# Two uneven groups of tokens, 384 and 512, in place of two batches of 448 in the two layers behind attention

## The chip, the cores and the metric

The kernel runs on one core of a Trainium2 chip. TensorE (PE in the profile) does the matmuls; VectorE (DVE), ScalarE (ACT) and GpSimd (POOL) do the work between them; SyncE (SP) issues the transfers. The metric is the device time of one execution in microseconds (us), lower is better.

## What is computed

Causal attention (2 batches, 12 heads, 448 positions, 64 wide) gives 896 tokens of 768 numbers. Two layers follow, on all 896 tokens:

```python
def _moe_ref(x, w_in, w_out, a, b):          # 768 -> 2048 -> 768
    h = x @ w_in
    P = a[0] + a[1] * h + a[2] * h**2 + a[3] * h**3
    Q = 1.0 + np.abs(b[0]) * np.abs(h) + np.abs(b[1]) * h**2
    return (P / (Q + 1e-06)) @ w_out

def _moe2_ref(x, w_gate, w_val, w_out):      # 768 -> 1536 -> 768
    gate = 1.0 / (1.0 + np.exp(-(x @ w_gate)))
    return (gate * (x @ w_val)) @ w_out
```

## The kernel before

Every number of the layers is kept as a high and a low part, and each product is three matmuls: high by high, high by low, low by high. A matmul has 128 x 128 weights (or, in the last product, 128 x 128 of the tokens' numbers) that stand still, and a moving operand of so many columns. For all products but the last the columns are tokens: 448 of them, one batch.

The first layer goes in four chunks `c` of 512 of the 2048 inner numbers. Stage in(c, b) makes four tiles `h` of 128 inner numbers for batch `b` (6 steps of 3 matmuls each, 72 in all, lines 239 to 241); the function `rational` then works on each tile on ACT and DVE, and POOL makes the low part `gl` (line 271). Stage out(c, b) multiplies them by `w_out` into six tiles `o` (4 steps of 3 matmuls each, 72 in all, lines 295 to 297), which DVE adds to the sums `y1` (line 305; in chunk 0 ACT copies them). After the last chunk ACT and POOL write the sums as `xh` and `xl`, the second layer's input.

The second layer goes in six chunks of 256 inner numbers. Stage in2(c, b) makes tiles `gu` (gate) and `vu` (value), 18 matmuls each, two of each kind per stage. Stage out2(c, b) makes tiles `z`, whose moving operand is 384 columns of weights, 6 matmuls each: six tiles for tokens 0 to 383 (b = 0), eight for the rest (b = 1).

The order of the work on each engine is written out by a planner: each piece is a `Job` with an engine, a cost, what it waits for and a rank, and `in_turn` plays them through. All matmuls stand in one chain, in the order of the stages: in(0,0), out(0,0), in(0,1), in(1,0), out(0,1), in(1,1), out(1,0), in(2,0) and so on to in(3,1), out(3,0); then in2(0,0) woven into out(3,1), in2(0,1), and from there out2(c,0), in2(c+1,0), out2(c,1), in2(c+1,1). Six PSUM banks take the matmuls' results in turn.

Of the kernel before, what the change touches and what calls it, by code (L numbers as in the profile page):

```python
# [69 lines left out]
def tile_causal_attention__moe_rational__moe_glu(  # L70
# [26 lines left out]
    NT = B * S  # L97
# [10 lines left out]
    tmp = ctx.enter_context(tc.tile_pool(name="tmp", bufs=3))  # L108
# [10 lines left out]
    for i in range(N_WARM):  # L119
# [7 lines left out]
        out=mask[:, S - CP :],  # L127
# [88 lines left out]
    YW = 4 * DM  # L216
    ypools = [y_a, None]

    ready = [0] + [(b + 1) * S // P for b in range(B)]
    y1 = {}  # L220
    y2 = {}
    wt = {}
# [4 lines left out]
    def psum_tile(nm, n=S):  # L227
        if "b" not in bank:
            return ps_a.tile([P, 512], F32, tag="mm", name=nm)[:, :n]
        nmm[0] += 1  # L230
        pool = ps_a if nmm[0] % 6 < 2 else bank["b"]
        return pool.tile([P, 512], F32, tag="mm", name=nm)[:, :n]

    def up(ps, w, fo, b):
        hi, lo = w
        bs = slice(b * S, (b + 1) * S)
        fs = slice(fo, fo + P)
        for c in range(KC):
            nc.tensor.matmul(ps, hi[:, c, fs], xh[:, c, bs], start=(c == 0), stop=False)  # L239
            nc.tensor.matmul(ps, hi[:, c, fs], xl[:, c, bs], start=False, stop=False)  # L240
            nc.tensor.matmul(ps, lo[:, c, fs], xh[:, c, bs], start=False, stop=(c == KC - 1))  # L241
            yield

    def rational(ps, gh, gl, nm):
        t = tmp.tile([P, S], F32, tag="t0", name=f"t_{nm}")
        z = tmp.tile([P, S], F32, tag="t1", name=f"z_{nm}")

        if "d" in bank:
            d = bank["d"].tile([P, 512], F32, tag="d", name=f"d_{nm}")[:, :S]
        else:  # L250
            d = tmp.tile([P, S], F32, tag="t2", name=f"d_{nm}", bufs=2)

        nc.scalar.activation(z, ps, AF.Square)
        nc.scalar.activation(d, ps, AF.Abs, scale=b_sb[:, 0:1])
        nc.scalar.activation(t, ps, AF.Identity, bias=a_sb[:, 2:3], scale=a_sb[:, 3:4])
        yield
        nc.vector.scalar_tensor_tensor(z, z, nb[:, 1:2], d, op0=ALU.mult, op1=ALU.subtract)
        nc.vector.tensor_tensor(t, t, ps, op=ALU.mult)
        nc.vector.scalar_tensor_tensor(t, t, a_sb[:, 1:2], ps, op0=ALU.add, op1=ALU.mult)
        yield  # L260

        nc.scalar.activation(d, z, AF.Ln, bias=one, scale=-1.0)
        nc.scalar.activation(d, d, AF.Exp, scale=-1.0)
        yield
        nc.vector.scalar_tensor_tensor(t, t, a_sb[:, 0:1], d, op0=ALU.add, op1=ALU.mult)
        nc.vector.scalar_tensor_tensor(d, z, one, d, op0=ALU.subtract, op1=ALU.mult)
        nc.vector.scalar_tensor_tensor(t, d, 2.0, t, op0=ALU.add, op1=ALU.mult)
        yield
        nc.scalar.copy(gh, t)  # L269
        yield  # L270
        nc.gpsimd.tensor_tensor(gl, t, gh, op=ALU.subtract)  # L271

    def in1_tile(c, b, i):

        nm = f"h{c}_{b}_{i}"
        if i % 2 == 0:
            for t in ("gh", "gl"):
                g[t, c, b, i // 2] = gpools[b].tile([P, 2, S], F32R, tag=t, name=f"{t}_{nm}")
        gh, gl = (g[t, c, b, i // 2][:, i % 2] for t in ("gh", "gl"))
        g[c, b, i] = gh, gl  # L280
        ps = psum_tile(nm)
        return up(ps, wt["in", c, i // 2], (i % 2) * P, b), rational(ps, gh, gl, nm)

    def out1_tile(c, b, e):

        if c == 0 and e == 0:
            y1[b] = ypools[b].tile([P, YW], F32, tag="y", name=f"y1_{b}")
        ps = psum_tile(f"o{c}_{b}_{e}")

        def products():  # L290
            es = slice(e * P, (e + 1) * P)
            for i in range(NF):
                hi, lo = wt["out", c, i]
                gh, gl = g[c, b, i]
                nc.tensor.matmul(ps, hi[:, es], gh, start=(i == 0), stop=False)  # L295
                nc.tensor.matmul(ps, hi[:, es], gl, start=False, stop=False)  # L296
                nc.tensor.matmul(ps, lo[:, es], gh, start=False, stop=(i == NF - 1))  # L297
                yield

        def follows():  # L300
            yy = y1[b][:, e * S : (e + 1) * S]
            if c == 0:
                nc.scalar.copy(yy, ps)
            else:
                nc.vector.tensor_tensor(yy, yy, ps, op=ALU.add)
            if c == NCH - 1:
                yield
                x = (slice(None), e, slice(b * S, (b + 1) * S))
                nc.scalar.copy(xh[x], yy)
                yield  # L310
                nc.gpsimd.tensor_tensor(xl[x], yy, xh[x], op=ALU.subtract)

        return products(), follows()

    def gate_tile(c, b, i):
        g["gate"] = psum_tile(f"gu{c}_{b}_{i}")
        return up(g["gate"], wt["gate", c, 0], i * P, b), None

    def val_tile(c, b, i):

        nm = f"u{c}_{b}_{i}"
        if b == 0:
            g["l2", c, i] = [gpools[c % 2].tile([P, NT], F32R, tag=t, name=f"{t}2_{c}_{i}") for t in ("gh", "gl")]
        gh, gl = (t[:, b * S : (b + 1) * S] for t in g["l2", c, i])
        pg = g["gate"]
        pv = psum_tile(f"v{nm}")

        def follows():
            sg = tmp.tile([P, S], F32, tag="t0", name=f"sg_{nm}")
            pr = tmp.tile([P, S], F32, tag="t1", name=f"pr_{nm}")  # L330
            nc.scalar.activation(sg, pg, AF.Sigmoid)
            yield
            nc.vector.tensor_tensor(pr, sg, pv, op=ALU.mult)  # L333
            yield
            nc.scalar.copy(gh, pr)  # L335
            yield
            nc.gpsimd.tensor_tensor(gl, pr, gh, op=ALU.subtract)  # L337

        return up(pv, wt["val", c, 0], i * P, b), follows()

    def out2_tile(c, m, n):

# [271 lines left out]

    job("late", "", 0.0, [k for k in J if k != "ab"], 0, late)

    UNIT, UNIT2 = 0.615, 0.52

    STAGES = [("SP", 4.0), ("ACT", 0.92), ("ACT", 0.9), ("DVE", 1.3), ("ACT", 0.84), ("POOL", 2.0)]
    portions = []  # L620
# [90 lines left out]
    GLU = [("ACT", 0.62), ("DVE", 0.62), ("ACT", 0.56), ("POOL", 1.25)]  # L711

    def stage_in(c, b):

        groups = [(0, 1), (2,), (3,)] if (c, b) == (0, 0) else [(i,) for i in range(NF)]
        for group in groups:
            keys = [("in", c, b, i) for i in group]
            deps = [place(k, 1) for k in keys]
            for u in range(KC):
                for k, d in zip(keys, deps):  # L720
                    w = [("in", c, k[3] // 2, u // 3, 5), ("lo", b * NP + u)]
                    matmuls(k, u, d + w, UNIT, in1_tile)
# [142 lines left out]
```

## Time and profile before

| | |
|---|---|
| time, median of 3 runs | 609.58 us (609.33 to 610.33) |
| the profiled execution | 614.51 us |
| its span, first to last instruction | 612.5 us |
| PE busy | 604.6 us, 99% of the span |
| DVE, ACT, POOL busy | 357.9, 356.8, 256.6 us |

The profiled execution is one, taken with the hardware profiler on, and 0.8% longer than the median; times inside the kernel come from it. An engine that is busy 99% of the span is not at its peak for that: matmuls are pipelined, and a matmul's listed duration overlaps the next one's.

### The profile page before, as it was taken

Reading aid. Unit: us, or ns where it says so; the run is one execution under the profiler, and the core shown is the slowest. Engines: PE = TensorE matmul, PEld = TensorE weight load, DVE = VectorE, ACT = ScalarE, POOL = GpSimd, SP = SyncE. Lnnn points to the kernel's source line nnn. Section 1 sums busy time; section 2 is a strip of 40 time slices with the busy share of each in tenths; the row PEclk is TensorE's granted clock in tenths of the full one; section 3 lists DMA queues with packets and bytes.
Section 4 is the critical chain, followed back from the end, with each engine's and each line's share of the span. In section 5 each row is a group of like instructions: output and inputs, shape, how many; then the busy total and the mean of one; then the engine's idle time right before and its main releaser. Section 6 shows DMA issues by size and latency. Waiting matters only on the chain.

```text
span 612.5 us, 8782 instructions
## 1 busy us (share of the span) xinstructions
PE 604.6 (99%) x3352; PEld 524.1 (86%) x3352; DVE 357.9 (58%) x659; ACT 356.8 (58%) x680; POOL 256.6 (42%) x187
## 2 busy tenths in 40 slices
PE   7999999999999999999999999999999999999997
PEld 5566666689999999999999999999999999999997
DVE  5877999839879686868794153335335336302314
ACT  6888888858888394959394348676335344110010
POOL 0634321377358535641856465636135144121010
PEclk9999999999999999999999999999999999999999
DMA  7645340154314341333231045645324133000004
GB/s 238 202 171 163 127 145 16 36 159 168 104 52 155 97 162 49 107 103 104 101 106 51 2 155 158 204 147 165 101 103 152 57 103 104 0 1 1 0 8 173
DMA packets 25641, 65.05 MB, mean 106 GB/s; under 512 B 1984, under 2 KB 3776, under 8 KB 25600
## 3 DMA queue, kind: packets, MB, share of 16 engines
q1 hardware_dynamic: 25600, 64.50, 32.3%
q8 instruction: 26, 0.43, 0.3%
q14 instruction: 15, 0.12, 0.1%
HBM read 61.74 MB, written 2.75 MB: 105 GB/s over the span
## 4 chain that ended last, share of the span: by engine, by line
PE 97%; DVE 2%; issue 0%; ACT 0%; DVEq 0%
PE h L239 7%; PE o L295 7%; PE h L240 6%; PE h L241 6%; PE o L296 6%; PE o L297 6%; PE vu L239 5%; PE vu L241 5%; PE gu L239 5%; PE gu L241 5%; PE vu L240 5%; PE gu L240 5%; PE z L355 5%; PE z L356 5%; PE z L357 5%; PE s L418 4%
## 5 line engine op out<-in xcount | busy, mean ns | idle before, releaser
L337 POOL TENSOR_TENSOR gl<-pr_u,gh 128x448 fp32r<-128x448 f32 x24 | 28.5, 1189 | 114.1 <-ACT gh L335 114.1
L271 POOL TENSOR_TENSOR gl_h<-t_h,gh_h 128x448 fp32r<-128x448 f32 x32 | 41.9, 1310 | 79.3 <-ACT gh_h L269 79.2
L239 PE MATMUL h<-xh,wh_in 128*128 128x448 f32 x192 | 72.2, 376 | 0.0
L295 PE MATMUL o<-gh_h,oh_out 128*128 128x448 f32 x192 | 71.2, 371 | 0.0
L297 PE MATMUL o<-gh_h,ol_out 128*128 128x448 f32 x192 | 70.6, 368 | 0.0
L296 PE MATMUL o<-gl_h,oh_out 128*128 128x448 f32 x192 | 70.6, 368 | 0.0
L241 PE MATMUL h<-xh,wl_in 128*128 128x448 f32 x192 | 70.6, 368 | 0.0
L240 PE MATMUL h<-xl,wh_in 128*128 128x448 f32 x192 | 70.6, 368 | 0.0
L176 POOL TENSOR_TENSOR ol_out<-val_out,oh_out 128x768 fp32r<-128x768 f32 x28 | 53.5, 1918 | 29.0 <-ACT oh_out L174 27.6
L333 DVE TENSOR_TENSOR pr_u<-sg_u,vu 128x448 f32<-128x448 f32 x24 | 14.8, 619 | 81.7 <-PE vu L241 76.9
L355 PE MATMUL z<-oh_out,gh 128*128 128x384 f32 x168 | 56.2, 334 | 0.0
L357 PE MATMUL z<-oh_out,gl 128*128 128x384 f32 x168 | 56.1, 334 | 0.0
L356 PE MATMUL z<-ol_out,gh 128*128 128x384 f32 x168 | 56.1, 334 | 0.0
L440 ACT ACTIVATE e<-e,sc 112x112 f32<-112x112 f32 (+3 forms) x96 | 49.7, 521 | 6.8 <-DVE sc L426 6.7
L365 DVE TENSOR_TENSOR y<-y,z 128x384 f32<-128x384 f32 x70 | 38.3, 552 | 26.2 <-PE z L357 25.8
L240 PE MATMUL gu<-xl,wh_gate 128*128 128x448 f32 x144 | 53.0, 368 | 0.0
L241 PE MATMUL gu<-xh,wl_gate 128*128 128x448 f32 x144 | 53.0, 368 | 0.0
L239 PE MATMUL vu<-xh,wh_val 128*128 128x448 f32 x144 | 53.0, 368 | 0.0
L240 PE MATMUL vu<-xl,wh_val 128*128 128x448 f32 x144 | 53.0, 368 | 0.0
L241 PE MATMUL vu<-xh,wl_val 128*128 128x448 f32 x144 | 53.0, 368 | 0.0
L239 PE MATMUL gu<-xh,wh_gate 128*128 128x448 f32 x144 | 52.9, 368 | 0.0
L164 DVE SCALAR_TENSOR_TENSOR val_out<-raw_out 128x768 uint32<-128x768 uint32 x28 | 34.0, 1215 | 26.4 <-ACT raw_out L161 23.9
(89 smaller groups left out, 1426.9 us busy)
## 6 DMA issues: line engine op xcount, KB each, us to landing
raw_out<-in_moe_w_out_dram SPq DMA_DIRECT2D x28, 768.0 KB, 4.2
raw_in<-in_moe_w_in_dram SPq DMA_DIRECT2D x16, 768.0 KB, 4.5
raw_gate<-in_moe_w_gate_dram SPq DMA_DIRECT2D x12, 768.0 KB, 4.4
raw_val<-in_moe_w_val_dram SPq DMA_DIRECT2D x12, 768.0 KB, 4.4
qk<-in_qk_dram SPq DMA_DIRECT2D x12, 448.0 KB, 5.6
v<-in_v_dram SPq DMA_DIRECT2D x12, 224.0 KB, 3.5
out_dram<-y SPq DMA_DIRECT2D x14, 192.0 KB, 1.8
a_sb<-in_moe_a_dram SPq DMA_DIRECT2D x1, 2.0 KB, 7.6
```

The costliest lines, as they stand in the source:

```text
L176: nc.gpsimd.tensor_tensor(lo, vf, hi, op=ALU.subtract)
L239: nc.tensor.matmul(ps, hi[:, c, fs], xh[:, c, bs], start=(c == 0), stop=False)
L240: nc.tensor.matmul(ps, hi[:, c, fs], xl[:, c, bs], start=False, stop=False)
L241: nc.tensor.matmul(ps, lo[:, c, fs], xh[:, c, bs], start=False, stop=(c == KC - 1))
L271: nc.gpsimd.tensor_tensor(gl, t, gh, op=ALU.subtract)
L295: nc.tensor.matmul(ps, hi[:, es], gh, start=(i == 0), stop=False)
L296: nc.tensor.matmul(ps, hi[:, es], gl, start=False, stop=False)
L297: nc.tensor.matmul(ps, lo[:, es], gh, start=False, stop=(i == NF - 1))
L355: nc.tensor.matmul(ps, gh[:, ms], hi[:, ns], start=(i == 0), stop=False)
L356: nc.tensor.matmul(ps, gh[:, ms], lo[:, ns], start=False, stop=False)
L357: nc.tensor.matmul(ps, gl[:, ms], hi[:, ns], start=False, stop=(i == NF2 - 1))
L440: nc.scalar.activation(e, e, AF.Exp, bias=d["sc"][:, t, j : j + 1], scale=-1.0, accum_out=d["sum"][:, t, j : j + 1])
```

## The change

Chunk 0 of the first layer keeps the two batches. From chunk 1 on, and in the whole second layer, the groups are tokens 0 to 383 (b = 0) and tokens 384 to 895 (b = 1). The sums `y1` keep their layout by batch, so a tile `o` of the second group, whose first 64 tokens belong to batch 0, is added in two pieces. The temporaries are 512 wide. The planner's costs follow the widths: 0.525 for three matmuls of 384 columns and 0.69 for three of 512, where 448 has 0.615.

```diff
+    CUT = S // P * P
+    ready = [0, CUT // P, NT // P]
+
+    def tokens(c, b):
+        return slice(b * S, (b + 1) * S) if c == 0 else (slice(0, CUT), slice(CUT, NT))[b]
+
+    def width(c, b):
+        ts = tokens(c, b)
+        return ts.stop - ts.start
+
+    def pieces(c, b):
+
+        ts = tokens(c, b)
+        for k in range(B):
+            lo, hi = max(ts.start, k * S), min(ts.stop, (k + 1) * S)
+            if lo < hi:
+                yield k, slice(lo - k * S, hi - k * S), slice(lo - ts.start, hi - ts.start)
...
-        t = tmp.tile([P, S], F32, tag="t0", name=f"t_{nm}")
-        z = tmp.tile([P, S], F32, tag="t1", name=f"z_{nm}")
+        n = ps.shape[-1]
+        t = tmp.tile([P, 512], F32, tag="t0", name=f"t_{nm}")[:, :n]
+        z = tmp.tile([P, 512], F32, tag="t1", name=f"z_{nm}")[:, :n]
...
-        ps = psum_tile(nm)
-        return up(ps, wt["in", c, i // 2], (i % 2) * P, b), rational(ps, gh, gl, nm)
+        ps = psum_tile(nm, n)
+        return up(ps, wt["in", c, i // 2], (i % 2) * P, tokens(c, b)), rational(ps, gh, gl, nm)
...
-            yy = y1[b][:, e * S : (e + 1) * S]
-            if c == 0:
-                nc.scalar.copy(yy, ps)
-            else:
-                nc.vector.tensor_tensor(yy, yy, ps, op=ALU.add)
+            parts = []
+            for k, ts, of in pieces(c, b):
+                yy = y1[k][:, e * S + ts.start : e * S + ts.stop]
+                if c == 0:
+                    nc.scalar.copy(yy, ps[:, of])
+                else:
+                    nc.vector.tensor_tensor(yy, yy, ps[:, of], op=ALU.add)
+                parts.append((yy, (slice(None), e, slice(k * S + ts.start, k * S + ts.stop))))
             if c == NCH - 1:
                 yield
-                x = (slice(None), e, slice(b * S, (b + 1) * S))
-                nc.scalar.copy(xh[x], yy)
+                for yy, x in parts:
+                    nc.scalar.copy(xh[x], yy)
                 yield
-                nc.gpsimd.tensor_tensor(xl[x], yy, xh[x], op=ALU.subtract)
+                for yy, x in parts:
+                    nc.gpsimd.tensor_tensor(xl[x], yy, xh[x], op=ALU.subtract)
...
-        return up(g["gate"], wt["gate", c, 0], i * P, b), None
+        return up(g["gate"], wt["gate", c, 0], i * P, tokens(1, b)), None
...
-    UNIT, UNIT2 = 0.615, 0.52
+    UNIT2 = 0.525
+    UNIT = {S: 0.615, CUT: 0.525, NT - CUT: 0.69}
```

`ready`, the count of 128-token blocks that the stages out2 may take after each group, stays 0, 3, 7. On PE no instruction changes its place; the widths change. PE at the end of in(1,1), before (an `h` or `o` is named by chunk, group and tile, and 128x448 is the result's size):

```order
L240 MATMUL h1_1_3_2170<-xl_118,wh_in1_1_1623 128x448
L241 MATMUL h1_1_3_2170<-xh_117,wl_in1_1_1624 128x448
L295 MATMUL o1_0_0_2209<-gh_h1_0_0_1778,oh_out1_0_2067 128x448
L296 MATMUL o1_0_0_2209<-gl_h1_0_0_1779,oh_out1_0_2067 128x448
L297 MATMUL o1_0_0_2209<-gh_h1_0_0_1778,ol_out1_0_2068 128x448
```

The same place on PE now:

```order
L257 MATMUL h1_1_3_2174<-xl_118,wh_in1_1_1623 128x512
L258 MATMUL h1_1_3_2174<-xh_117,wl_in1_1_1624 128x512
L314 MATMUL o1_0_0_2203<-gh_h1_0_0_1778,oh_out1_0_2075 128x384
L315 MATMUL o1_0_0_2203<-gl_h1_0_0_1779,oh_out1_0_2075 128x384
L316 MATMUL o1_0_0_2203<-gh_h1_0_0_1778,ol_out1_0_2076 128x384
```

The second group's tiles have 512 columns and the first group's 384; nothing else moved. DVE in out(1,1), before:

```order
L305 TENSOR_TENSOR y1_1_1920<-y1_1_1920,o1_1_0_2466 128x448
L257 SCALAR_TENSOR_TENSOR z_h2_0_2_2485<-z_h2_0_2_2485,nb_114,d_h2_0_2_2486 128x448
L258 TENSOR_TENSOR t_h2_0_2_2484<-t_h2_0_2_2484,h2_0_2_2401 128x448
L259 SCALAR_TENSOR_TENSOR t_h2_0_2_2484<-t_h2_0_2_2484,a_sb_112,h2_0_2_2401 128x448
L305 TENSOR_TENSOR y1_1_1920<-y1_1_1920,o1_1_1_2493 128x448
```

DVE at the same place now:

```order
L275 SCALAR_TENSOR_TENSOR z_h2_0_2_2471<-z_h2_0_2_2471,nb_114,d_h2_0_2_2472 128x384
L276 TENSOR_TENSOR t_h2_0_2_2470<-t_h2_0_2_2470,h2_0_2_2402 128x384
L277 SCALAR_TENSOR_TENSOR t_h2_0_2_2470<-t_h2_0_2_2470,a_sb_112,h2_0_2_2402 128x384
L326 TENSOR_TENSOR y1_0_1300<-y1_0_1300,o1_1_0_2466 128x64
L326 TENSOR_TENSOR y1_1_1911<-y1_1_1911,o1_1_0_2466 128x448
L164 SCALAR_TENSOR_TENSOR val_out2_1_2519<-raw_out2_1_2433 128x768
L326 TENSOR_TENSOR y1_0_1300<-y1_0_1300,o1_1_1_2496 128x64
L326 TENSOR_TENSOR y1_1_1911<-y1_1_1911,o1_1_1_2496 128x448
```

Each tile `o` of the second group has two adds, of 64 and of 448 columns, and the adds and the work of `rational` and of the weights change places by one or two. ACT and POOL change in the same way; SP's transfers keep their order. One thing more shows in what PE waits for: sixteen tiles' first matmuls now wait for a count of PE itself. One tile is shown, before and then now, PE in in(2,1):

```order
L239 MATMUL h2_1_1_2629<-xh_117,wh_in2_0_1706 128x448
L256 MATMUL h2_1_1_2637<-xh_117,wh_in2_0_1706 128x512 [waits PE_49]
```

Before the change one tile of the two layers, the fifth of out(0,0), has such a wait.

## Rows read from the trace of the kernel before

**Rows 1.** The page's first part: busy us (share of the span) xinstructions.
```profile
PE 604.6 (99%) x3352; PEld 524.1 (86%) x3352; DVE 357.9 (58%) x659; ACT 356.8 (58%) x680; POOL 256.6 (42%) x187
```
**Rows 2.** The page's fourth part: the chain that ended last, by engine.
```profile
PE 97%; DVE 2%; issue 0%; ACT 0%; DVEq 0%
```
**Rows 3.** Groups by line on PE: busy us, mean ns | idle us before.
```profile
L241 PE MATMUL h<-xh,wl_in 128*128 128x448 f32 x192 | 70.6, 368 | 0.0
...
L297 PE MATMUL o<-gh_h,ol_out 128*128 128x448 f32 x192 | 70.6, 368 | 0.0
...
L355 PE MATMUL z<-oh_out,gh 128*128 128x384 f32 x168 | 56.2, 334 | 0.0
...
L241 PE MATMUL vu<-xh,wl_val 128*128 128x448 f32 x144 | 53.0, 368 | 0.0
```
**Rows 4.** Busy time of each engine in two stretches, the layers one and two.
```profile
core 0: us, PE busy (x) PEld busy (x) DVE busy (x) ACT busy (x) POOL busy (x), PEclk, DMA share, GB/s
122.00:372.00 250.00, 250.00 (x1216) 226.31 (x1217) 174.25 (x243) 167.34 (x276) 142.34 (x101) 1.00 0.33 107
372.00:612.00 240.00, 236.97 (x1228) 223.00 (x1227) 86.09 (x117) 89.33 (x132) 74.21 (x47) 1.00 0.28 91
```
**Rows 5.** Timeline of PE, in2(1,1) and out2(1,0): start us, us, what.
```profile
402.29 0.37 PE L240 MATMUL gu<-xl,wh_gate 128*128 128x448 f32 x1
...
416.96 0.34 PE L355 MATMUL z<-oh_out,gh 128*128 128x384 f32 x1
417.14 0.33 PE L356 MATMUL z<-ol_out,gh 128*128 128x384 f32 x1
...
423.21 0.36 PE L239 MATMUL gu<-xh,wh_gate 128*128 128x448 f32 x1
```
**Rows 6.** Groups by line of the weight loads (PEld).
```profile
L241 PEld LDWEIGHTS h<-xh,wl_in 128*128 128x128 f32 x192 | 36.0, 188 | 3.5
...
L355 PEld LDWEIGHTS z<-oh_out,gh 128*128 128x128 f32 x168 | 31.5, 188 | 0.2
```
**Rows 7.** Timeline of PE, a short run of 448-column matmuls between attention's.
```profile
97.15 0.37 PE L240 MATMUL h<-xl,wh_in 128*128 128x448 f32 x1
97.36 0.36 PE L241 MATMUL h<-xh,wl_in 128*128 128x448 f32 x1
97.56 0.37 PE L239 MATMUL h<-xh,wh_in 128*128 128x448 f32 x1
...
98.57 0.36 PE L241 MATMUL h<-xh,wl_in 128*128 128x448 f32 x1
```
**Rows 8.** Groups by line on DVE, ACT and POOL.
```profile
L305 DVE TENSOR_TENSOR y<-y,o 128x448 f32<-128x448 f32 x36 | 22.2, 620 | 23.1 <-PE o L297 22.9
...
L426 DVE CUSTOM_DVE_ANT_0 e<-s,mask 112x112 f32<-112x112 f32 x24 | 5.6, 271 | 8.9 <-PE s L418 8.9
L446 DVE TENSOR_SCALAR sum<-sum 112x8 f32<-112x8 f32 x12 | 3.8, 314 | 0.6 <-ACT e L440 0.5
...
L269 ACT CAST gh_h<-t_h 128x448 fp32r<-128x448 f32 x32 | 18.2, 570 | 17.6 <-DVE t_h L267 17.6
```
**Rows 9.** Timelines of POOL and PE: last gl and its reader, three places.
```profile
160.19 1.16 POOL L271 TENSOR_TENSOR gl_h<-t_h,gh_h 128x448 fp32r<-128x448 f32 x1 [1.66 <-ACT gh_h L269]
...
166.39 0.37 PE L296 MATMUL o<-gl_h,oh_out 128*128 128x448 f32 x1
...
323.60 1.16 POOL L271 TENSOR_TENSOR gl_h<-t_h,gh_h 128x448 fp32r<-128x448 f32 x1 [0.39 <-ACT gh_h L269]
...
330.07 0.37 PE L296 MATMUL o<-gl_h,oh_out 128*128 128x448 f32 x1
...
595.84 1.16 POOL L337 TENSOR_TENSOR gl<-pr_u,gh 128x448 fp32r<-128x448 f32 x1 [6.29 <-ACT gh L335]
...
601.36 0.33 PE L357 MATMUL z<-oh_out,gl 128*128 128x384 f32 x1
```
**Rows 10.** Timelines of POOL and PE: the last out weights of chunk 3.
```profile
309.16 1.86 POOL L176 TENSOR_TENSOR ol_out<-val_out,oh_out 128x768 fp32r<-128x768 f32 x1
...
315.40 0.37 PE L297 MATMUL o<-gh_h,ol_out 128*128 128x448 f32 x1
```
**Rows 11.** Timeline of PE around the fifth tile of out(0,0).
```profile
129.40 0.37 PE L297 MATMUL o<-gh_h,ol_out 128*128 128x448 f32 x1
129.60 0.37 PE L295 MATMUL o<-gh_h,oh_out 128*128 128x448 f32 x1
129.81 0.37 PE L296 MATMUL o<-gl_h,oh_out 128*128 128x448 f32 x1
```

More of the change, by code (lines that the diff above doesn't have):

```diff
@@ L217, in tile_causal_attention__moe_rational__moe_glu @@
     ypools = [y_a, None]
-    ready = [0] + [(b + 1) * S // P for b in range(B)]
+    CUT = S // P * P
[11 more added lines that the diff above has]
+                yield k, slice(lo - k * S, hi - k * S), slice(lo - ts.start, hi - ts.start)
     y1 = {}
@@ L232, in psum_tile, with up @@
         return pool.tile([P, 512], F32, tag="mm", name=nm)[:, :n]
-    def up(ps, w, fo, b):
+    def up(ps, w, fo, bs):
         hi, lo = w
-        bs = slice(b * S, (b + 1) * S)
         fs = slice(fo, fo + P)
@@ L244, in rational @@
     def rational(ps, gh, gl, nm):
-        t = tmp.tile([P, S], F32, tag="t0", name=f"t_{nm}")
-        z = tmp.tile([P, S], F32, tag="t1", name=f"z_{nm}")
+        n = ps.shape[-1]
+        t = tmp.tile([P, 512], F32, tag="t0", name=f"t_{nm}")[:, :n]
+        z = tmp.tile([P, 512], F32, tag="t1", name=f"z_{nm}")[:, :n]
         if "d" in bank:
-            d = bank["d"].tile([P, 512], F32, tag="d", name=f"d_{nm}")[:, :S]
+            d = bank["d"].tile([P, 512], F32, tag="d", name=f"d_{nm}")[:, :n]
         else:
-            d = tmp.tile([P, S], F32, tag="t2", name=f"d_{nm}", bufs=2)
+            d = xn_p.tile([P, S], F32, tag="d", name=f"d_{nm}", bufs=2)
         nc.scalar.activation(z, ps, AF.Square)
@@ L277, in in1_tile @@
             for t in ("gh", "gl"):
-                g[t, c, b, i // 2] = gpools[b].tile([P, 2, S], F32R, tag=t, name=f"{t}_{nm}")
-        gh, gl = (g[t, c, b, i // 2][:, i % 2] for t in ("gh", "gl"))
+                g[t, c, b, i // 2] = gpools[b].tile([P, 2, (S, 512)[b]], F32R, tag=t, name=f"{t}_{nm}")
+        n = width(c, b)
+        gh, gl = (g[t, c, b, i // 2][:, i % 2, :n] for t in ("gh", "gl"))
         g[c, b, i] = gh, gl
-        ps = psum_tile(nm)
-        return up(ps, wt["in", c, i // 2], (i % 2) * P, b), rational(ps, gh, gl, nm)
+        ps = psum_tile(nm, n)
+        return up(ps, wt["in", c, i // 2], (i % 2) * P, tokens(c, b)), rational(ps, gh, gl, nm)
     def out1_tile(c, b, e):
@@ L287, in out1_tile @@
             y1[b] = ypools[b].tile([P, YW], F32, tag="y", name=f"y1_{b}")
-        ps = psum_tile(f"o{c}_{b}_{e}")
+        ps = psum_tile(f"o{c}_{b}_{e}", width(c, b))
         def products():
@@ L300, in follows @@
         def follows():
-            yy = y1[b][:, e * S : (e + 1) * S]
-            if c == 0:
-                nc.scalar.copy(yy, ps)
-            else:
-                nc.vector.tensor_tensor(yy, yy, ps, op=ALU.add)
+            parts = []
[6 more added lines that the diff above has]
+                parts.append((yy, (slice(None), e, slice(k * S + ts.start, k * S + ts.stop))))
             if c == NCH - 1:
                 yield
-                x = (slice(None), e, slice(b * S, (b + 1) * S))
-                nc.scalar.copy(xh[x], yy)
+                for yy, x in parts:
+                    nc.scalar.copy(xh[x], yy)
                 yield
-                nc.gpsimd.tensor_tensor(xl[x], yy, xh[x], op=ALU.subtract)
+                for yy, x in parts:
+                    nc.gpsimd.tensor_tensor(xl[x], yy, xh[x], op=ALU.subtract)
         return products(), follows()
     def gate_tile(c, b, i):
-        g["gate"] = psum_tile(f"gu{c}_{b}_{i}")
-        return up(g["gate"], wt["gate", c, 0], i * P, b), None
+        g["gate"] = psum_tile(f"gu{c}_{b}_{i}", width(1, b))
+        return up(g["gate"], wt["gate", c, 0], i * P, tokens(1, b)), None
     def val_tile(c, b, i):
@@ L323, in val_tile @@
             g["l2", c, i] = [gpools[c % 2].tile([P, NT], F32R, tag=t, name=f"{t}2_{c}_{i}") for t in ("gh", "gl")]
-        gh, gl = (t[:, b * S : (b + 1) * S] for t in g["l2", c, i])
+        n = width(1, b)
+        gh, gl = (t[:, tokens(1, b)] for t in g["l2", c, i])
         pg = g["gate"]
-        pv = psum_tile(f"v{nm}")
+        pv = psum_tile(f"v{nm}", n)
         def follows():
-            sg = tmp.tile([P, S], F32, tag="t0", name=f"sg_{nm}")
-            pr = tmp.tile([P, S], F32, tag="t1", name=f"pr_{nm}")
+            sg = tmp.tile([P, 512], F32, tag="t0", name=f"sg_{nm}")[:, :n]
+            pr = tmp.tile([P, 512], F32, tag="t1", name=f"pr_{nm}")[:, :n]
             nc.scalar.activation(sg, pg, AF.Sigmoid)
@@ L337, in follows @@
             nc.gpsimd.tensor_tensor(gl, pr, gh, op=ALU.subtract)
-        return up(pv, wt["val", c, 0], i * P, b), follows()
+        return up(pv, wt["val", c, 0], i * P, tokens(1, b)), follows()
     def out2_tile(c, m, n):
@@ L711, in tile_causal_attention__moe_rational__moe_glu, with scaled @@
     GLU = [("ACT", 0.62), ("DVE", 0.62), ("ACT", 0.56), ("POOL", 1.25)]
+    def scaled(stages, c, b, more=0.0):
+        f = width(c, b) / S
+        return [(engine, (cost - 0.15) * f + 0.15 + more) for engine, cost in stages]
     def stage_in(c, b):
@@ L721, in stage_in @@
                     w = [("in", c, k[3] // 2, u // 3, 5), ("lo", b * NP + u)]
-                    matmuls(k, u, d + w, UNIT, in1_tile)
+                    matmuls(k, u, d + w, UNIT[width(c, b)], in1_tile)
             for k in keys:
-                followed(k, RATIONAL, ("out", c, b, 0, "mm", k[3]))
+                followed(k, scaled(RATIONAL, c, b), ("out", c, b, 0, "mm", k[3]))
             yield
@@ L734, in stage_out @@
             for i in range(NF):
-                matmuls(key, i, deps + [("out", c, i, 0, 5), ("in", c, b, i, "after", 5)], UNIT, out1_tile)
-            follow(key, stages, at["end"] + R_SUM)
+                matmuls(key, i, deps + [("out", c, i, 0, 5), ("in", c, b, i, "after", 5)], UNIT[width(c, b)], out1_tile)
+            follow(key, scaled(stages, c, b, 0.15 * (c > 0) * b), at["end"] + R_SUM)
             yield
@@ L745, in stage_in2 @@
                     w = [(key[0], c, 0, u // 3, 5), ("out", NCH - 1, b, u, "after", 2)]
-                    matmuls(key, u, deps + w, UNIT, make)
-            followed(kv, GLU, ("out2", c, ready[b], 0, "mm", i), [("in", NCH - 1, 1, NF - 1, "after", 2)])
+                    matmuls(key, u, deps + w, UNIT[width(1, b)], make)
+            followed(kv, scaled(GLU, 1, b), ("out2", c, ready[b], 0, "mm", i), [("in", NCH - 1, 1, NF - 1, "after", 2)])
             yield
```

## The prediction

> **What bounds the kernel now.** I read the page's busy times first: PE is busy 604.6 of 612.5 us, the others 58% or less [rows 1]. The chain that ended last is 97% PE [rows 2], and the groups of the two layers' matmuls show no idle time ahead of them [rows 3]. The granted clock is 1.00 in both layers, its upper level of 2.4 GHz, and DVE, ACT and POOL have at least 75 of 250 us free in layer one and 150 of 240 in layer two [rows 4]. So from 122 us on the time is the sum of the distances from one matmul's start to the next one's, and only two things can move it: that distance, or a wait that PE does not have today.
>
> The distance is not the mean of a group (368 and 334 ns), since matmuls overlap; it is counted from the timeline [rows 5]. Stage in2(1,1) has 72 matmuls of 448 columns; from the second, at 402.29, to the first z at 416.96 are 71: 14.67 / 71 = 206.6 ns. Stage out2(1,0) has 36 of 384 columns; from the second, at 417.14, to the next gu at 423.21 are 35: 6.07 / 35 = 173.4 ns. At 2.4 GHz, 448 columns are 186.7 ns and 384 are 160.0, so the excess is 19.9 and 13.4 ns: neither nothing nor a constant per matmul. The weight load listed with each matmul lasts 188 ns at either width [rows 6], longer than the 173.4 at which z matmuls follow each other, so it runs beside them and doesn't set the distance alone. h, o, vu and z differ in operands, but the three 448-wide kinds have one mean [rows 3], so I take the distance to hang on the number of columns.
>
> **The change part by part.**
>
> *Widths.* Stages of 72 matmuls: in and out of chunks 1 to 3 (6 for each group) and in2 of six chunks (6 for each group). That is 12 x 72 = 864 matmuls of the first group that go from 448 to 384 columns, and 864 of the second that go from 448 to 512. Per pair: 413.2 ns before, 173.4 + T now, where T is the distance of 512-column matmuls. No row shows T. The gain is 864 x (239.8 ns - T), so everything hangs on it. By rows:
> - a straight line through both widths (33.2 ns for 64 columns) gives T = 239.8, and the gain is nothing;
> - the excess of 384 columns, 213.3 + 13.4, gives T = 226.7: 864 x 13.1 = 11.3 us;
> - between attention's matmuls the 448-wide ones come closer together: seven from 97.15 to 98.57 [rows 7], 202.9 ns each, 0.453 ns per column, and 384-wide ones need 173.4 / 384 = 0.452. One price per column gives T = 231.2: 7.4 us;
> - in the long runs the excess looks like two and three steps of some 6.65 ns. A price of 0.452 per column would ask for 15.6 ns of excess at 448, 2.3 steps, and three are paid; at 512 it asks for 17.8, 2.7 steps, and three would be 213.3 + 20.0 = 233.3: 864 x 6.5 = 5.6 us.
>
> I take the last: it is the one reading in which the steady 448, the loose 448 and the 384 all agree. The ends, 226.7 and 239.8, stay for the range.
>
> *What does not move.* Attention, chunk 0 (288 matmuls of 448 columns) and all z keep widths and places; PE's and SP's programs keep their order.
>
> *The split adds.* Chunks 1 to 3 have 6 tiles each with a second DVE add of 64 columns: 18 more, and after chunk 3 six more ACT casts and six more POOL subtractions. A 64-column add has no row: at most the 620 ns of a 448-column one, at least the 271 to 314 ns of the small DVE instructions [rows 8]. I take 0.3 us, 18 x 0.3 = 5.4 us of DVE, beside PE, out of 75.8 us that DVE has free in layer one [rows 4]. Uncovered it would cost these 5.4 us; it is late only for the PSUM bank of its tile, which comes round five tiles later, 10 us or more.
>
> *Elementwise work.* Each instruction of rational and of the gates covers 384 or 512 columns instead of 448, 14% less or more: the sum is the same, but the second group's chains end later.
>
> *Handoffs that get tighter.* The last gl of in(3,1) ends at 323.60 + 1.16 = 324.76, and PE reads it at 330.07 [rows 9]: 5.3 us of cover. Between them lies out(3,0), which shrinks by 72 x 33.2 ns = 2.4 us, and the chain's last steps (three DVE instructions of some 620 ns and a cast of 570 [rows 8], POOL's 1.16 us [rows 9], together 3.6 us) get 14%, 0.5 us, longer: 2.4 us stay. For in(0,1) the gl ends at 161.35 and is read at 166.39: 5.0 us, less 2.4 for in(1,0), stays 2.6, as its own chain keeps 448 columns. At the end gl ends at 597.00 and is read at 601.36 [rows 9]: out2(5,0) between them keeps its length, so 4.4 us less some 0.3 stay. The out weights of chunk 3, ready at 311.02 for 315.40 [rows 10], gain cover, because in(3,1) ahead of them grows by 72 x 26.7 ns = 1.9 us. All cost nothing as long as cover is left; where it is gone every later matmul shifts, since all stand behind the waiting one in PE's queue.
>
> *PE waiting for itself.* Sixteen tiles begin with such a wait. If each waited for the matmul just ahead to end, it would cost 368 - 207 = 161 ns, 2.6 us in all. The one tile that has such a wait today starts at 129.60, after 129.40 and before 129.81, the usual distance [rows 11], so I take nothing.
>
> *Sum.* 614.51 us of the profiled execution less 5.6 is 608.9, 0.91% less; the median of 609.58 less 0.91% is 604.0 us.
>
> **The rivals.**
>
> *No change: the distance is a straight line* (T near 240). For it: two points always lie on a line, and the excess does grow with the width. Against: a line through both meets zero columns at -25.8 ns, and the loose 448 at 202.9 lies below it. Time 609.6 us. The Trainium skill's page "TensorE: Matmul & The Clock Gate" has a rule of the same outcome in "Back-to-back issue gap": once warm, columns / 2.4 + 2.5 ns. By it a pair costs 378.4 ns before and after, and uneven groups give nothing. The trace disagrees with its sizes (206.6 and 173.4 measured, 189.2 and 162.5 by the rule).
>
> *A small excess at 512* (T = 226.7 or a little less): the excess would follow not the width but whether columns come in whole multiples of 128, as 384 and 512 do and 448 does not. For it: 384 has the smaller excess, and nothing else in the rows tells 448 from it. Against: only two widths are seen. Time 609.58 - 11.2 = 598.4 us.
>
> *Slower: the excess grows faster than the width.* 13.4, 19.9, and then two steps more, 33 ns: T = 246.6, and the time is 609.58 + 864 x 6.8 ns x 0.99 = 615.4 us. It decides from T = 239.8 upwards. For it: the step from 384 to 448 is already more than in proportion, and 512 columns fill a whole tile of PSUM. Against: the loose 448s, which show that the third step is not needed by every matmul.
>
> *A handoff runs out.* DVE or ACT work, in its new order, delays a second group's gl by more than 2.4 us in in(3,1) or in(0,1), or all sixteen self-waits are paid: about 2 us, 606 us. For it: the covers of 2.4 and 2.6 us are the smallest of layer one. Against: DVE is idle 30% of that layer [rows 4].
>
> That the widths do not change at all is excluded by the order of PE's instructions.
>
> **How the numbers follow.** The forecast, T from 231 to 235, has 0.48; the straight line 0.20; the small excess 0.15, and still less 0.04; the growing excess 0.07; a handoff 0.06. The predicted time is the forecast's, 604.0 us, with 601.9 to 605.7 as its own range. The range over the cases runs from the small excess to the straight line, 598.0 to 609.8, and leaves out the growing excess, what lies below 598 and a part of the line's scatter, some 0.17. A measurement of this kernel can tell about 0.2% from no change, 1.2 us. Faster by more: the forecast, both small excesses and the handoff, 0.73. The straight line splits into 0.17 within 0.2% and 0.03 slower through small waits; with the growing excess slower has 0.10.
>
> **What the profile will show.** Right: in a stage of the second group 72 matmuls take 16.8 us (233.3 ns each) and one of the first 12.5 us; layer two's in2 stages thus 29.3 us a chunk where they take 29.8; no idle time ahead of h, o, gu, vu and z; DVE adds of 64 columns near 0.3 us with PE not waiting. Wrong: 17.3 us for the second group's stage (straight line), 16.3 (small excess), 17.8 (growing), or PE rows with idle time behind gl or behind a PSUM bank at out(0,1) or out(3,1). What would make the prediction wrong is T alone by 5 us either way; a handoff could take 2.

## The result, and the profile after

The changed kernel takes 603.67 us (median of 4 runs, 603.26 to 604.00) against 609.48 us (609.33 to 610.33): a ratio of 0.9900, 95% interval 0.9889 to 0.9912. The profiled execution of after takes 603.39 us, in line with its other runs. That of before took 614.51 us, 5 us above its own median, so the two profiles lie 11.1 us apart where the medians lie 5.8 apart; the first experiment shows what the other 5 us are.

The page's first and fourth part say that nothing has changed in kind; they answer to [rows 1] and [rows 2]:

```profile
PE 593.5 (99%) x3352; PEld 511.6 (85%) x3352; DVE 358.0 (60%) x677; ACT 357.2 (59%) x686; POOL 254.4 (42%) x193
...
PE 97%; DVE 2%; issue 0%; ACT 0%; DVEq 0%
```

Busy time in the stretches of the two layers, as in [rows 4]; the granted clock is 1.00 in both, the upper level:

```profile
core 0: us, PE busy (x) PEld busy (x) DVE busy (x) ACT busy (x) POOL busy (x), PEclk, DMA share, GB/s
122.00:372.00 250.00, 250.00 (x1252) 225.48 (x1249) 175.51 (x263) 174.57 (x292) 144.76 (x109) 1.00 0.34 110
372.00:602.00 230.00, 225.89 (x1191) 211.34 (x1189) 84.60 (x114) 82.34 (x122) 69.67 (x46) 1.00 0.27 90
```

The timeline of PE around in2(1,1) and in2(2,0), the places of [rows 5]:

```profile
393.07 0.39 PE L256 MATMUL gu<-xh,wh_gate 128*128 128x512 f32 x1
...
409.43 0.33 PE L379 MATMUL z<-oh_out,gh 128*128 128x384 f32 x1
...
415.70 0.33 PE L256 MATMUL gu<-xh,wh_gate 128*128 128x384 f32 x1
...
428.18 0.33 PE L379 MATMUL z<-oh_out,gh 128*128 128x384 f32 x1
```

A stage of 72 matmuls of 512 columns takes 409.43 - 393.07 = 16.36 us, 227.2 ns each; one of 384 takes 428.18 - 415.70 = 12.48 us, 173.3 ns each. In other stages, in(2,1) for one, 72 take 16.32 us, 226.7 ns each. Of the four values that the prediction set out for the wide stage (16.3, 16.8, 17.3, 17.8 us) the first is the one that came: the small excess, which it had given 0.15. A pair costs some 400.6 ns.

### The profile page after: what moved, and what is told of

The parts are those of the page before. It is cut to its first block, busy times and chain, and to the rows that moved or that the text cites. A ratio compares the mean times of both kernels' runs of the same rounds, so it can differ in the third digit from the quotient of the medians.

```text
span 601.4 us, 8821 instructions
## 1 busy us (share of the span) xinstructions
PE 593.5 (99%) x3352; PEld 511.6 (85%) x3352; DVE 358.0 (60%) x677; ACT 357.2 (59%) x686; POOL 254.4 (42%) x193
## 4 chain that ended last, share of the span: by engine, by line
PE 97%; DVE 2%; issue 0%; ACT 0%; DVEq 0%
PE h L256 7%; PE o L314 6%; PE h L258 6%; PE h L257 6%; PE o L315 6%; PE o L316 6%; PE z L381 5%; PE z L379 5%; PE z L380 5%; PE gu L257 5%; PE gu L258 5%; PE gu L256 5%; PE vu L257 5%; PE vu L256 5%; PE vu L258 5%; PE s L442 4%
## 5 line engine op out<-in xcount | busy, mean ns | idle before, releaser
L256 PE MATMUL h<-xh,wh_in 128*128 128x384 f32 (+2 forms) x192 | 71.3, 371 | 0.0
L314 PE MATMUL o<-gh_h,oh_out 128*128 128x384 f32 (+2 forms) x192 | 70.3, 366 | 0.0
L315 PE MATMUL o<-gl_h,oh_out 128*128 128x384 f32 (+2 forms) x192 | 69.9, 364 | 0.0
L316 PE MATMUL o<-gh_h,ol_out 128*128 128x384 f32 (+2 forms) x192 | 69.9, 364 | 0.0
L258 PE MATMUL h<-xh,wl_in 128*128 128x384 f32 (+2 forms) x192 | 69.7, 363 | 0.0
L257 PE MATMUL h<-xl,wh_in 128*128 128x384 f32 (+2 forms) x192 | 69.7, 363 | 0.0
L258 PE MATMUL gu<-xh,wl_gate 128*128 128x384 f32 (+1 forms) x144 | 52.2, 363 | 0.0
L257 PE MATMUL gu<-xl,wh_gate 128*128 128x384 f32 (+1 forms) x144 | 52.2, 363 | 0.0
L257 PE MATMUL vu<-xl,wh_val 128*128 128x384 f32 (+1 forms) x144 | 52.1, 362 | 0.0
L256 PE MATMUL gu<-xh,wh_gate 128*128 128x384 f32 (+1 forms) x144 | 52.1, 362 | 0.0
```

## The experiments

The kernel before ran beside every one of these: 610.08 us in the runs of the first eight (with the changed kernel once more among them, below), 610.05 us in those of the last four.

### The kernel before once more

No edit.

> The kernel before, unchanged. The profiled execution of before took 614.51 us with 448-column matmuls 206.6 ns apart, but its median is 609.5. Theory V: the distance of 448-column matmuls differs between executions of one program; in an execution of 609.5 us the span is near 607.5 and the 448-column matmuls of both layers are 203 to 205 ns apart on average, the 384-column ones 173.4 as always. Theory F: the 448s are always 206.6 ns apart, and the 5 us lie in one place elsewhere (attention, a wait, the end); then a new profile shows 206.6 again.

609.96 us (609.11 to 610.21, 12 runs). This time the profiled execution, 610.21 us, is an ordinary one. Timeline of PE, stages in2(0,1) and in2(1,1):

```profile
353.77 0.36 PE L239 MATMUL gu<-xh,wh_gate 128*128 128x448 f32 x1
...
368.36 0.34 PE L355 MATMUL z<-oh_out,gh 128*128 128x384 f32 x1
...
397.83 0.36 PE L239 MATMUL gu<-xh,wh_gate 128*128 128x448 f32 x1
...
412.70 0.34 PE L355 MATMUL z<-oh_out,gh 128*128 128x384 f32 x1
```

The same 72 matmuls of 448 columns take 14.59 us (202.7 ns each) before the first z and 14.87 us (206.6 ns) behind it. So it is throughout: from in(0,1) on every stage up to 368.36 goes at 202.7 ns, every stage between two runs of z at 206.6. In the execution of [rows 5] layer one went at 206.7 too; its stage in(3,1), 72 matmuls in 14.88 us:

```profile
298.24 0.37 PE L239 MATMUL h<-xh,wh_in 128*128 128x448 f32 x1
...
313.12 0.37 PE L295 MATMUL o<-gh_h,oh_out 128*128 128x448 f32 x1
```

One width, two distances, 4 ns apart: over the some 1,200 such matmuls from 125 us to the first z that is 4.7 us, nearly all of the 5.0 by which that execution exceeds the median. So theory V holds for layer one; layer two has 206.6 in both executions. Of the 29 executions of the kernel before that ran beside the last four experiments, 4 took 614.5 to 614.9 us and the others at most 610.7.

### The two layers apart

Uneven groups in layer two alone: in the second layer `width("two", b)` and `tokens("two", b)` stand for `width(1, b)` and `tokens(1, b)`, and

```diff
-        return slice(b * S, (b + 1) * S) if c == 0 else (slice(0, CUT), slice(CUT, NT))[b]
+        return (slice(0, CUT), slice(CUT, NT))[b] if c == "two" else slice(b * S, (b + 1) * S)
```

> Groups of 384 and 512 in the second layer alone (432 of the 864 pairs), batches of 448 in all of the first. If the gain is a sum over pairs (6.7 ns each by the medians: 5.8 us / 864), half of it remains: 2.9 us less than before, 606.6 us. If it came from the first layer or from fewer waits there, nothing: 609.5 us. In the trace 512-column matmuls are 226.7 ns apart, 384-column ones 173.4.

605.47 us (605.28 to 605.51, 6 runs), ratio 0.9910 (0.9880 to 0.9939): 4.6 us of the gain are layer two's, more than the half that was expected. Its pairs go from 413.2 to 400.6 ns, and the five chunks behind the first z have 360 of them: 4.5 us.

### Other cuts

Only the cut and the planner's costs for the two widths change:

```diff
-    CUT = S // P * P
+    CUT = 416
```

> The changed kernel with the cut at 416: groups of 416 and 480 columns, the same sum, neither a multiple of 128. Theory M (widths that are whole multiples of 128 pay 13.3 ns over columns at 2.4 GHz, others more, up to 20): 416 at 193 and 480 at 220 ns, 413 a pair, no gain in an execution where the 448s are 206.6 apart; 609 to 612 us. Theory P (what I predicted: a price per column of 0.452 ns, rounded up to steps of 6.7 ns): 416 is 188.0, paid as 186.7 or 193.3 (excess 14.7 is 2.2 steps, 3 paid: 193.3), 480 is 217.0 (excess 17.0, 2.6 steps, 3 paid: 220.0): the same numbers; the width sweep tells these two apart, this run tells whether evenness as such costs (a straight line: no change from 448 and 448).

607.12 us (606.28 to 609.31, 12 runs), ratio 0.9943 (0.9921 to 0.9965): half the gain, which neither theory gave. From stage to stage 416 columns take 186.7 or 188.4 ns and 480 take 213.3 to 220.0, so that these widths too have more than one distance, the shortest of them columns / 2.4 + 13.3 ns; the mean pair is 187.9 + 217.3 = 405.2 ns. The mean pair of the kernel before, in an ordinary execution, is (504 x 405.4 + 360 x 413.2) / 864 = 408.7, and 864 x 3.5 ns = 3.0 us is the gain seen.

With `CUT = 400` in the same place:

> The changed kernel with the cut at 400: groups of 400 and 496 columns. By the width sweep both lie outside the band of 416 to 480 (180.0 and 220.0 ns, 400.0 a pair, as 384 and 512): the same time as the changed kernel within 0.5 us, 603.7. If it took whole multiples of 128 it would cost what the cut at 416 costs, 607 us.

609.34 us (608.62 to 610.19, 11 runs), ratio 0.9992 (0.9984 to 1.0001): no change. The sweep below gave 400 and 496 columns 180.0 + 220.0 ns, as good a pair as 384 and 512. In the kernel the narrow stages keep that (180.0 to 180.4, but for out(1,0), whose 72 take 14.76 us), and the wide ones, at 223.2 to 226.7, don't. Timeline of PE, stage in2(0,1):

```profile
354.08 0.38 PE L256 MATMUL gu<-xh,wh_gate 128*128 128x496 f32 x1
...
370.40 0.34 PE L379 MATMUL z<-oh_out,gh 128*128 128x384 f32 x1
```

16.32 us / 72 = 226.7 ns for 496 columns: what 512 cost. So a width's distance from a sweep did not carry over, and the kernel had to be timed. The widths are not all of it: out(1,0) is 1.8 us longer than the other narrow stages, with a wait in it that the changed kernel has not, here from PE's list (us in total, times, longest):

```profile
PE o L316 <- POOL ol_out L176: 1.3, 1, 1.3
```

Without it a mean pair is 180.1 + 225.8 = 405.9 ns, 2.8 less than before, which makes 2.4 us; less 1.8 that leaves 0.6, and 0.7 was measured.

### Widths by themselves

In place of the kernel, matmuls from one set of weights and one of columns, 12 to a PSUM tile and 72 to a width. It leaves out attention and both layers.

```diff
+    for n in (256, 288, 320, 352, 384, 400, 416, 432, 448, 464, 480, 496, 512):
+        for _ in range(6):
+            group(n, 0)
...
+    for lead in (128, 176, 224, 304, 336, 368):
+        group(lead, 0, 1)
+        for _ in range(6):
+            group(448, 0)
```

> Left out: the whole computation. One core runs only matmuls of the same number format, 72 in a row at each width from 256 to 512 columns (12 to a PSUM tile), then 384, 448 and 512 from other offsets, then 448s six times behind one short matmul of another width each. Theory M: the excess over columns / 2.4 GHz is 13.3 ns at 384 and 512 (and some such value at 256) and larger in between. Theory P: the excess grows with steps: 2 steps to about 400, 3 at 432 and more, 3 at 512 (20 ns): refuted already by the changed kernel's 226.7 unless it differs here. Theory L (straight line): 64 more columns always cost 33 ns. The six runs of 448s show whether the distance can lie at 200 to 203 or 206.7 from the same widths, by what came before them.

Mean distance between starts, counted in the trace, and its excess over columns / 2.4:

```
columns   256   320   352   384   400   416   432   448   464   480   496   512
ns      120.0 146.7 160.0 173.3 180.0 188.4 195.7 202.7 209.0 216.8 220.0 226.7
excess   13.3  13.3  13.3  13.3  13.3  15.0  15.7  16.0  15.6  16.8  13.3  13.3
```

(288 columns: 131.7 and 11.7.) The excess doesn't grow with the width: in this sweep it is 13.3 ns at nearly all, and 15 to 17 from 416 to 480. Behind a stage of 384 columns, 144 matmuls of 448, which read from two other places of the columns, took 206.6 ns each instead of 202.7. One single matmul put ahead of 72 others of 448, all from the first place, then decided which of the two it was: 202.7 behind 224 and 368 columns (and, after the first twelve or so, behind 128), 206.7 behind 176, 304 and 336. The first of these leads stood behind 512s, the others behind 448s.

A second sweep took widths in between, weights of 64 and 96 columns in place of 128, and more leads, now behind runs of 384; it leaves out the same.

```diff
+    for m in (64, 96):
+        for n in (256, 320, 384, 416, 448, 480, 512):
...
+    for lead in (32, 64, 96, 160, 192, 256, 288, 320, 352, 400):
+        for _ in range(2):
+            group(384, 0)
+        group(lead, 0, 1)
+        for _ in range(4):
+            group(448, 0)
```

> Left out: the whole computation. Only matmuls, 48 in a row. First the edges of the band: 404, 408, 412 and 484, 488, 492 columns. Then weights of 64 and of 96 columns in place of 128. Theory W: the extra time between 416 and 480 columns comes of the weight load (listed at 188 ns; with 128 weight columns the matmuls are 188 ns apart just at 416), so with fewer weight columns the load is shorter and the band moves to fewer columns or goes. Theory N: it hangs on the moving columns alone and stays at 416 to 480 whatever the weights. Last, 448s behind two tiles of 384 and one short matmul of another width each: they settle at 202.7 or at 206.7 ns; if what comes before sets it, both values appear over the ten widths.

The widths in between: 404, 408 and 412 columns took 182.2, 185.0 and 186.6 ns, excesses of 13.9 to 15.0; 484, 488 and 492 took 218.7, 225.7 and 222.3, excesses of 17.0 to 22.4. So the band does not end at 416 and 480. With half the weights, whose loads are listed at 134 ns in place of 188, 384 columns take 173.3 ns and 448 take 202.2, as with 128: the length of the weight load does not set the distance at these widths, though it is not without effect at others (at 256 columns it goes from 120.0 to 113.4, at 512 from 226.7 to 230.0). With weights of 96 columns, 384 take 175.0, 448 take 202.6 and 512 take 230.0. Behind 384s, a lead of 256, 288 or 320 columns gave 202.5 to 202.6 ns over the next 48 matmuls of 448. Behind leads of 192 and less the first twelve went at 204.5 to 209.6 and the others at 202.6 to 202.8; leads of 352 and 400 columns gave 206.4 and 206.6.

### A lead ahead of the 448s

The sweep's finding put to the kernel before, whose widths stay: one matmul more, whose product is overwritten, ahead of each of layer two's ten stages that follow a run of z.

```diff
+        if c > 0 and i == 0:
+            hi, _ = wt["gate", c, 0]
+            nc.tensor.matmul(g["gate"][:, :256], hi[:, 0, :P], xh[:, 0, :256], start=True, stop=True)
```

> The kernel before, widths unchanged, with ten matmuls added: one of 256 columns, whose product is overwritten, ahead of the first gate matmul of each group of chunks 1 to 5 of layer two, which is the first 448-column matmul behind a run of z. Theory A (the distance of 448 columns is set by what runs just before a stage: 206.7 ns behind 384 columns, 202.7 behind a lead of 256): the ten stages of 72 fall from 206.6 to 202.7 ns, 10 x 72 x 3.95 = 2.8 us less, and the leads cost 10 x 0.117 = 1.2 us: 1.6 us faster although it does more work. Theory B (206.6 ns belongs to layer two, by its operands or its place): 1.2 us slower.

> As the run with a lead of 256 columns, but the ten added matmuls have 352. Theory A: behind a lead of 352 the 448-column matmuls stay at 206.6 ns, so only the leads' own 10 x 0.159 us are seen: 1.6 us slower than before, 3.2 us slower than with leads of 256. Theory B: 1.6 us slower than before too, but 0.4 us slower than with leads of 256.

608.55 us (608.25 to 613.60) with leads of 256 columns, 611.64 us (610.67 to 616.54) with 352, 12 runs each: 3.1 us between two kernels that differ only in the width of ten matmuls. Timelines of PE, stage in2(1,0), first with 256:

```profile
374.51 0.28 PE L319 MATMUL gu<-xh,wh_gate 128*128 128x256 f32 x1
374.63 0.37 PE L239 MATMUL gu<-xh,wh_gate 128*128 128x448 f32 x1
...
389.22 0.34 PE L358 MATMUL z<-oh_out,gh 128*128 128x384 f32 x1
```

and with 352:

```profile
373.66 0.32 PE L319 MATMUL gu<-xh,wh_gate 128*128 128x352 f32 x1
373.82 0.36 PE L239 MATMUL gu<-xh,wh_gate 128*128 128x448 f32 x1
...
388.69 0.34 PE L358 MATMUL z<-oh_out,gh 128*128 128x384 f32 x1
```

14.59 us behind the one, 14.87 behind the other, in all ten stages. Theory A holds and B falls: in layer two the 206.6 ns do not come of the operands but of what runs just ahead of the stage. 384 columns are not the only way to them, since layer one has them throughout in the execution of [rows 5], with no 384s ahead. Against before, 608.55 is unclear by its interval (ratio 0.9989, 0.9959 to 1.0019), because both kernels have some executions 5 us up; the other 8 of 12 runs lie at 608.25 to 608.67, below every run of before (609.24 and up).

### Chunks 1 and 2 alone

`if c in (1, 2)` in place of `if c == "two"` in the diff on the layers apart: 288 pairs are uneven, all else is 448.

> The change in chunks 1 and 2 of layer one alone: 288 pairs of 384 and 512 columns, everything else 448. By the widths alone (400.1 to 400.9 ns for a pair in place of 405.4): 288 x 4.5 to 5.3 = 1.3 to 1.5 us faster than before. By theory A the 448-column stages that follow a stage of 384 fall to 206.7 ns, as out(0,1) does in the changed kernel, and those behind them stay there: out(0,1), in(3,0) and up to five more stages x 72 x 4 ns = 0.6 to 2.0 us given back, so between 0.9 us faster and 0.7 us slower.

609.26 us (608.72 to 610.74, 12 runs), ratio 0.9974 (0.9952 to 0.9996): 0.8 us, less than the 1.4 that the widths alone would give. Timeline of PE, where the uneven stages end and meet 448s: in(3,0) behind 384 columns, out(2,1), in(3,1) behind 512.

```profile
264.69 0.36 PE L256 MATMUL h<-xh,wh_in 128*128 128x448 f32 x1
...
279.57 0.40 PE L314 MATMUL o<-gh_h,oh_out 128*128 128x512 f32 x1
...
295.94 0.36 PE L256 MATMUL h<-xh,wh_in 128*128 128x448 f32 x1
...
310.53 0.36 PE L314 MATMUL o<-gh_h,oh_out 128*128 128x448 f32 x1
```

14.88 us behind 384 columns, 14.59 behind 512, for the same 72 matmuls of the same kind: the mechanism once more, where nobody had put a lead. out(0,1), behind 384s, pays it here and in the changed kernel as well (14.87 us for 14.59); 1.4 less 0.3 for each of the two stages is the 0.8 seen.

### The side terms

The changed kernel with four adds for each of the 18 split ones of 64 columns:

```diff
+                    for _ in range(3 if of.stop - of.start < S // 2 else 0):
+                        nc.vector.tensor_tensor(spare, yy, ps[:, of], op=ALU.add)
```

> The changed kernel with each of the 18 split adds of 64 columns preceded by three more of the same kind into a spare tile: 54 x 0.22 = 11.9 us of DVE work more, beside PE. If the split adds lie beside PE (the prediction's term of nothing): 603.5 us, no change against the changed kernel. If they stand on the path, or if DVE's order delays a gl: 4 to 12 us slower.

603.39 us (602.90 to 604.34, 5 runs): 11.9 us more of DVE work cost nothing.

The changed kernel once more, and with chunk 0 in uneven groups too:

```diff
-        return slice(b * S, (b + 1) * S) if c == 0 else (slice(0, CUT), slice(CUT, NT))[b]
+        return (slice(0, CUT), slice(CUT, NT))[b]
```

> The changed kernel, unchanged, beside the others on one chip: 603.3 to 604.0 us as before, with 1.8 to 2.0 us outside its span, whatever state its few 448s are in (288 of them, at most 1.1 us between the states).

> The changed kernel with the groups of 384 and 512 in chunk 0 as well, so that no matmul of the two layers has 448 columns. If a matmul costs its columns at 2.4 GHz plus 13.3 ns at 384 and 512, and 448s cost 202.7 to 206.6, 144 pairs give 5 to 13 ns each: 0.8 to 1.9 us less than the changed kernel, 602 to 603 us. Against: in chunk 0 DVE and ACT are the busiest of the whole kernel, and in(0,0) fills PE's gaps between attention's matmuls, where fewer columns are worth nothing; then it is the same within 0.5 us.

The changed kernel: 603.49 us (603.20 to 603.75). With chunk 0: 605.69 us (604.38 to 607.02, 6 runs), 2.2 us slower, though 144 pairs more are uneven. PE's list of waits has four rows that the changed kernel's has not; the two longest are

```profile
PE o L314 <- ACT gh_h L287: 0.9, 1, 0.9
PE o L315 <- POOL gl_h L289: 0.7, 1, 0.7
```

In chunk 0 the stage out(0,0) waits for `rational`, at 120.1 and 121.3 us. The last matmul starts at 598.57 us, against 597.55 and 597.89 in the changed kernel's two profiles. Three of its six executions, of which there is no trace, are another 2.5 us longer, at a mean granted clock of 0.996 to 0.997 where the others show 0.999; where that falls stays open. No version beat the changed kernel by more than the runs can tell.

## Why the prediction was right, by two errors that nearly cancel

The time fell into the forecast's own range, but the distance of 512 columns did not fall between its 231 and 235 ns: that the time came out was luck.

**What bounds the kernel: right.** Groups of PE by form, as in [rows 3], with no idle time:

```profile
L381 PE MATMUL z<-oh_out,gl 128*128 128x384 f32 x168 | 56.2, 335 | 0.0
...
L258 PE MATMUL gu<-xh,wl_gate 128*128 128x512 f32 x72 | 28.1, 391 | 0.0
...
L316 PE MATMUL o<-gh_h,ol_out 128*128 128x512 f32 x72 | 28.1, 390 | 0.0
...
L258 PE MATMUL h<-xh,wl_in 128*128 128x512 f32 x72 | 28.0, 390 | 0.0
...
L258 PE MATMUL h<-xh,wl_in 128*128 128x384 f32 x72 | 24.1, 334 | 0.0
```

**The distance of 512 columns: wrong in size.** The prediction took 233.3 ns, "the one reading in which the steady 448, the loose 448 and the 384 all agree"; it is 226.7 in steady running and 227.4 as a mean of all 864. The reading in steps that grow with the width, and the price per column, are not borne out: the excess is 13.3 ns in the first sweep at 352, 384, 400, 496 and 512 columns alike, and 448 is an odd one. The rival of the small excess had the right number with too narrow a condition, since 352 and 400 are no multiples of 128.

**The pairs of before: wrong too.** 413.2 ns was put on all 864 pairs. That holds for the execution of [rows 5]. In ordinary ones only the 360 pairs behind a run of z cost it; the other 504 cost 405.4. The clue stood in [rows 7]: the loose 448s at 202.9 ns were the second distance, which the prediction read as a law of width. Scaling 614.51 to the median by its ratio hid the same error: the 5 us between the two do not lie evenly over the span but nearly all in layer one's 448s.

Put right, the sum is 504 x 4.8 + 360 x 12.6 ns = 7.0 us, less 0.3 for out(0,1) and 0.3 for the handoff below: 6.4 us. The medians give 5.8, those of the repeated runs 610.08 - 603.49 = 6.6, and the profiles of the two repeated runs 610.21 - 603.73 = 6.5, of which layer two has 4.8, layer one 1.5 and the time ahead of them 0.2, by their stages. The prediction's 5.6 us came of taking half a pair's gain (6.5 ns for 12.6) and of counting that pair 864 times, where only 360 gain 12.6 and the others 4.8: the one error made the gain too small, the other too large. The small excess, with the right distance and the wrong pairs, gave 598.4, 5.3 us too low.

The growing excess is excluded (17.8 us a stage forecast, 16.36 measured), the straight line too (17.3), and with it the outcome of the rule that the prediction quoted from the Trainium skill, page "TensorE: Matmul & The Clock Gate", section "Back-to-back issue gap", where it stands as the gap of an isolated matmul: its sizes are 162.5 and 215.8 ns for 384 and 512 columns, the trace has 173.3 and 226.7. Its form, columns / 2.4 plus a constant, does fit both widths, with 13.3 ns for the constant; 448 is what departs from it, and that is the gain.

**The split adds: right.** 221 ns each where 0.3 us was estimated, 4.0 us in all. Groups of DVE by form:

```profile
L326 DVE TENSOR_TENSOR y<-y,o 128x448 f32<-128x448 f32 x18 | 11.0, 614 | 0.0
...
L326 DVE TENSOR_TENSOR y<-y,o 128x64 f32<-128x64 f32 x18 | 4.0, 221 | 18.2 <-PE o L316 18.1
```

Four times as many stayed hidden, so DVE's free time in layer one is cover indeed.

**The handoffs: two right, one wrong.** For in(0,1), 2.6 us were to stay: gl ends at 160.70 and is read at 163.49, 2.8 us. At the end 4.1 stay, as forecast. For in(3,1) the prediction kept 2.4 us, and nothing is left. Timelines of ACT, POOL, PEld and PE there:

```profile
308.00 0.33 PE L314 MATMUL o<-gh_h,oh_out 128*128 128x384 f32 x1
...
308.80 0.91 ACT L161 ACTIVATE raw_out<-raw_out 128x768 uint32<-128x768 uint32 x1
310.89 0.52 ACT L331 CAST xh<-y 128x384 fp32r<-128x384 f32 x1 [1.18 <-DVE y L326]
311.31 0.62 ACT L287 CAST gh_h<-t_h 128x512 fp32r<-128x512 f32 x1
311.83 0.59 ACT L271 ACTIVATE z_h<-h 128x512 f32<-128x512 f32 x1
...
321.53 1.30 POOL L289 TENSOR_TENSOR gl_h<-t_h,gh_h 128x512 fp32r<-128x512 f32 x1 [0.82 <-ACT gh_h L287]
...
322.89 0.19 PEld L315 LDWEIGHTS o<-gl_h,oh_out 128*128 128x128 f32 x1 [0.34 <-POOL gl_h L289]
...
322.89 0.50 PE L315 MATMUL o<-gl_h,oh_out 128*128 128x512 f32 x1
```

The weight load waits 0.34 us, and out(3,1)'s first half takes 8.41 us where its second takes 8.20. The step that failed is "the chain's last steps ... get 14%, 0.5 us, longer: 2.4 us stay", which counted those last steps alone. Their length was right: from the first of the three DVE instructions to the end of gl it is 4.2 us where it was 3.8. But the chain on the last tile also starts later: ACT's first step on the last tile (L271, 311.83) comes 3.8 us after in(3,1) has given way to out(3,0) at 308.00, since ACT's order now has the cast of out(3,0)'s first tile ahead of it and waits 1.18 us for that tile's add. In the kernel before the same step (L253) came 2.0 us behind, in timelines of PE and ACT:

```profile
313.12 0.37 PE L295 MATMUL o<-gh_h,oh_out 128*128 128x448 f32 x1
...
315.08 0.57 ACT L253 ACTIVATE z_h<-h 128x448 f32<-128x448 f32 x1
```

And between that step and the last ones the chain takes 6.8 us in place of 5.9. So the 5.3 us of cover lose 2.4 by out(3,0), 0.5 by the last steps, both forecast, and 1.9 and 0.8 that were not: 0.3 us too few. That the order on ACT costs the 1.9 is read from the trace; no run tried another order. This is the rival of the handoff, at 0.3 us instead of 2, and not what decides.

**PE waiting for itself: right.** No such wait is in PE's list, and the stages have no time for it.

## What to carry to other kernels

Where matmuls stand back to back, their price is the distance between starts, by width and by what ran just before; two widths from one trace don't give a third, and even a sweep of that width alone can miss (496 columns: 220.0 ns in the sweep, 226.7 in the kernel). Look first how the profiled execution stands to the median, and where in the span the difference lies, before a sum is scaled from one to the other: here the 5 us were nearly all in layer one's 448s, most of which the change takes away. And where a gain comes from a width's odd price, a part of it can be had by other means, such as ten small matmuls more, and that makes a good test of the cause.

## What the runs showed that was not expected

- A run of 448-column matmuls keeps one of two distances, 202.7 or 206.6 ns, for as long as it lasts, but for its first matmuls behind some leads. Behind 384 columns, and behind 384s with a lead of 352 or 400, it was the longer; behind 512 columns, and behind 384s with a lead of 32 to 320, the shorter. Behind 448s a lead of 304 columns gave the longer and one of 368 the shorter, so the width of the matmul just ahead does not decide it alone. In the kernel before, layer one takes the shorter in one trace and the longer in the other; by their times, most executions of this one program are of the first kind and some of the second.
- In the sweeps, widths from 408 to 492 columns pay 15 to 22 ns over columns / 2.4 GHz, and most others 13.3. In the kernel 416 and 480 were also seen at 13.3, and 496 at 17 to 20. What in the engine makes the band and the several distances of one width is open; the length of the weight load alone does not, since half the weights changed neither 384 nor 448.
- More work made the kernel before faster in its ordinary executions: ten matmuls of 0.12 us each took 0.28 us from each of ten stages.
